# Value products by blocks of 32 queries, each with its own 128 keys, in an attention and feed-forward kernel

## The chip, the cores and the metric

The kernel runs on one core of one Trainium2 chip. The metric is the device time of one execution in microseconds (us); lower is better. The core's engines are named as the profile names them: PE (matrix products; PEld is its loading of the stationary operand), DVE and ACT (elementwise work), POOL (next to nothing here) and SP, which issues the DMA transfers here.

## The reference

Inputs and outputs are fp32. There are 8 batches of 8 heads, 512 local positions, 32 global positions, and 64 numbers per head.

```python
k_all = np.concatenate([k_g, k_l], axis=2); v_all = np.concatenate([v_g, v_l], axis=2)
out_g = np.matmul(sm(scale * np.matmul(q_g, k_all.transpose(0, 1, 3, 2))), v_all)
mask = np.abs(pos[:, None] - pos[None, :]) <= 32
s_ll = np.where(mask, scale * np.matmul(q_l, k_l.transpose(0, 1, 3, 2)), -1000000000.0)
s_lg = scale * np.matmul(q_l, k_g.transpose(0, 1, 3, 2))
a_l = sm(np.concatenate([s_lg, s_ll], axis=-1))
out_l = np.matmul(a_l, v_all)
x = np.concatenate([out_g, out_l], axis=2)        # then heads side by side: 4352 rows of 512
h = np.maximum(x @ w_in, 0.0)                     # 512 -> 2048
return h * h @ w_out                              # 2048 -> 512
```

`sm` is a softmax over the last axis. A local query sees the local keys at a distance of at most 32 and the 32 global keys. A global query sees all 544 keys.

## The kernel before, in words

**Heads and steps.** A "head" t of the kernel is one half (256 queries) of one head of one batch: 128 of them, in groups of 8 (`g = t // 8`); `hf = (t // 8) % 2` says which half of the sequence. The loop at L552 runs over steps t. Step t does the later part of head t, the scores of head t + 1 (`begin`, `rise`), and one step `m = t - 9` of the feed-forward part: `gemm1(m)` (24 passes into `h`), the square of the ReLU (`act1`, `act2`: `r`, `gh`, `gl`) and `gemm2(m - 1)` (24 passes into `o`). There are 17 blocks of 256 rows with 8 such steps each.

**Layout of one head.** The 256 queries are two sets u = 0, 1 of 128, and each set has a window of 224 key columns: 192 near keys and the 32 global ones, so that all columns of both windows are used. Before, the sets share the middle 64 near keys and the global keys: the row order of the keys is near 0 to 192, global, near 192 to 320, and set u takes columns 128u to 128u + 224. `raw` holds keys and queries (set u in partitions 64u to 64u + 64), `prob[t % 2]` the probabilities (128 queries x 2 x 224).

**Value products before.** `transposes` turns `prob` into `pt` by CHUNKS of keys: each set's own 128 keys, and the 96 shared keys (64 near, 32 global) of each set. `pt_evac` copies the 256 columns of `pt[0]` with ACT and of `pt[1]` with DVE to `pts`. `av` works on a pair of heads at each odd step: one product of the 96 shared keys with all 256 queries, and one product of 128 own keys for each set. The two heads of the pair write partitions 0 to 64 and 64 to 128 of `xa`, so they use the two halves of PE's columns. `x_evac` takes `xa` to `x_h` and `x_l`, the operands of `gemm1`.

**Global queries.** `g_scores` multiplies 32 global queries with each head's keys; `g_copy` (ACT) and `g_add` (DVE) put the scores in `sg`, two pieces per head where hf is 0 and three (128, 32 and 96 wide) where hf is 1. After a batch's half of heads come `g_soft` to `g_x`.

**Split numbers.** From head 16 on (`plain(t)` false) an fp32 operand is two operands (`hi`, `lo`; `x_h`, `x_l`; `gh`, `gl`) in a faster format, and three products replace one. The weights are loaded as pairs of 32-bit words (`wr`, 32 chunks of 512 KB), turned to fp32 (`wf`: ACT, then two DVE instructions each, in `w_bits`), and later split (`ws`). PLAN says in which of the first 24 steps these jobs are issued; `gemm1(m)` and `gemm2(m)` for m < 8 need the four `wf` chunks 4m to 4m + 3.

**Order.** PE's instructions stand in program order from the start, those of DVE and ACT from step 17 on (FREE). Before that, and for SP all along, a scheduler orders them by its own estimate of times. All loads go through one queue on SP: head t + 4's `raw` and `v` are asked for at step t (`load_head`), with 4 buffers for `raw` and 7 for `v`. A load waits on SP until the last use of the buffer it takes, and what stands behind it on SP waits too.

All calls of the engines go through `InOrder`, so the profile puts them under L53; groups are told apart by their tiles' names.

Of the kernel before, what the change touches and what calls it, by code (L numbers as in the profile page):

```python
# [7 lines left out]
F32 = mybir.dt.float32  # L8
# [6 lines left out]
B, H, SL, SG, D = 8, 8, 512, 32, 64  # L15
DM, DFF = 512, 2048
P = 128
HALF = 256
NGR = 2 * B
NT = NGR * H  # L20
WIN = 224
QK = WIN + P
VC = 192
NEG = -1.6e10
# [4 lines left out]
SCALE = 0.125  # L29
CHUNKS = ((0, 128), (320, 128), (128, 96), (224, 96))  # L30

# [28 lines left out]
def attention_moe(  # L60
# [10 lines left out]
    nc = tc.nc  # L71
    pe, ve, ac = InOrder(tc, nc.tensor), InOrder(tc, nc.vector), InOrder(tc, nc.scalar)
# [5 lines left out]
    pp = ctx.enter_context(tc.tile_pool(name="pp", bufs=3))  # L78
# [3 lines left out]
    pq = ctx.enter_context(tc.tile_pool(name="pq", bufs=4))  # L82
    pv = ctx.enter_context(tc.tile_pool(name="pv", bufs=7))

    heads = {}
# [9 lines left out]
    def load_head(t):  # L95
        raw = pq.tile([P, QK], F32, tag="raw", name=f"raw{t}")
        v = pv.tile([P, VC], F32, tag="v", name=f"v{t}")
        nc.sync.dma_start(raw, qk[t])
        nc.sync.dma_start(v, vv[t])
        heads[t] = dict(raw=raw, v=v)  # L100

# [17 lines left out]
    ident, masks = con[:, :P], con[:, P:]  # L119
# [58 lines left out]

    def g_parts(t):
        h4, grp = t % 4, (t // 4) % 2  # L180
        s = heads[t]["s"]
        if (t // 8) % 2 == 0:
            parts = ((0, 0, 0, 128), (1, 0, 128, 160))
        else:
            parts = ((0, 0, 288, 128), (1, 0, 416, 32), (1, 64, 448, 96))
        r = slice(32 * h4, 32 * h4 + 32)
        return [(sg[r, grp, d : d + n], s[u][:, WIN + o : WIN + o + n]) for u, o, d, n in parts]

    def g_copy(t):
        h4 = t % 4  # L190
        r = slice(32 * h4, 32 * h4 + 32) if plain(t) else slice(32, 64)
        for dst, src in g_parts(t):
            ac.copy(dst, src[r])

    def g_add(t):
        if plain(t):
            return
        for dst, src in g_parts(t):
            ve.tensor_add(dst, src[:32], dst)

# [50 lines left out]

    def av(t):
        pair = [heads[t], heads[t + 1]]
        for i in range(3):
            for e, hd in enumerate(pair):
                v, pts, o = hd["v"], hd["pts"], xa[half(e), :HALF]
                if i == 0:
                    pe.matmul(o, v[:96, 128:192], pts[:96, 2:4, :], start=True, stop=False, skip_group_check=True)
                else:
                    u = i - 1  # L260
                    pe.matmul(
                        o[:, P * u : P * u + P],
                        v[:, half(u)],
                        pts[:, u, :],
                        start=False,
                        stop=i == 2,
                        skip_group_check=True,
                    )

# [282 lines left out]
    for t in range(NSTEP + LAG + 1):  # L552
        m = t - LAG
        ve.on, ac.on, pe.on = [t >= x for x in FREE]
        prev, run, live, more = 1 <= t <= NT, 0 <= m < NSTEP, t < NT, t + 1 < NT
        pair = t - 3 if t % 2 and 3 <= t <= NT + 1 else None
        if t + 4 < NT:
            load_head(t + 4)
        if t % 4 == 0 and t + 4 < NT:
            g_load(t + 4)  # L560
# [37 lines left out]
        if live and t % 4 == 3 and (t // 8) % 2 == 1:  # L598
            d = t if t % 8 == 3 else t + 1
# [101 lines left out]
```

## Time and profile before

| | us |
|---|---|
| median of 3 runs (1072.8 to 1074.93) | 1072.96 |
| profiled execution | 1072.53 |
| its span, first to last instruction | 1070.7 |
| PE busy in the span | 1038.6 |
| DVE busy | 665.9 |
| ACT busy | 545.4 |

A row of the timeline has start, time covered, engine, line, operation, output and inputs, and the count of instructions; what stands in brackets is how long the engine was idle before it, and who ended that. The trace shows an fp32 product as two passes (two loads and two matmuls). Instructions on different parts of PE run side by side, so the time covered by several is less than the sum of their durations. A row of the chain has start, duration and what ran.

### The profile page before, as it was taken

The numbers are of one execution on the slowest core, as the hardware profiler recorded it, in microseconds if no ns is written. First come the engines' busy times: TensorE is split into PE (matmuls) and PEld (weight loads), VectorE is DVE, ScalarE is ACT, GpSimd is POOL, SyncE is SP. The second block draws the span as 40 slices with busy tenths as digits, with TensorE's granted clock in tenths as the row PEclk, the third lists the DMA queues.
The fourth block names the chain that finished last, engine by engine and source line by source line (L and its number), as shares of the span: only waits on it lengthen the run. The fifth ranks groups of instructions, "written<-read, shape, count | busy, mean of one in ns | idle before, by whom it ended". The sixth has DMA issues, their size and how long they took to land.

```text
span 1070.7 us, 21923 instructions
## 1 busy us (share of the span) xinstructions
PE 1038.6 (97%) x8320; PEld 868.7 (81%) x8320; DVE 665.9 (62%) x2340; ACT 545.4 (51%) x1617; POOL 0.5 (0%) x5
## 2 busy tenths in 40 slices
PE   5899889999999999999999999999999999999998
PEld 4766678888888888888888888888888888888897
DVE  5895576666666666666666666666666666653321
ACT  5886555555455445555454555554555554542222
POOL 0000000000000000000000000000000000000000
PEclk9899899999999999999999999999999999999999
DMA  8891111221221221122211221212221221101000
GB/s 266 300 331 50 51 55 42 62 61 58 66 65 36 63 83 46 58 63 62 66 58 38 69 74 46 66 44 74 66 62 39 69 73 46 39 1 45 1 21 21
DMA packets 72458, 75.88 MB, mean 71 GB/s; under 512 B 6304, under 2 KB 63776, under 8 KB 72352
## 3 DMA queue, kind: packets, MB, share of 16 engines
q1 hardware_dynamic: 72352, 74.47, 23.0%
q8 instruction: 66, 1.08, 0.4%
q14 instruction: 40, 0.33, 0.1%
HBM read 65.54 MB, written 8.91 MB: 70 GB/s over the span
## 4 chain that ended last, share of the span: by engine, by line
DVE 38%; PE 28%; ACT 24%; issue 7%; DMA 1%; SPq 0%; ACTq 0%
PE h L53 12%; PE o L53 11%; DVE prob L53 8%; ACT prob L53 7%; DVE r L53 6%; DVE gl L53 6%; ACT gh L53 5%; ACT r L53 5%; ACT sg L53 4%; DVE st L53 4%; DVE lo L53 4%; DVE pts L53 3%; PE xa L53 2%; DVE xg L53 2%; PE sb L53 2%
## 5 line engine op out<-in xcount | busy, mean ns | idle before, releaser
L53 PE MATMUL h<-x_h,ws 128*128 128x256 f32 x2048 | 401.7, 289 | 3.1 <-DVE r L53 3.1
L53 PEld LDWEIGHTS h<-x_h,ws 128*128 128x128 f32 x2048 | 327.9, 192 | 19.3 <-DVE r L53 5.6
L53 PE MATMUL o<-ws,gh 128*128 128x512 f32 x1024 | 321.3, 394 | 5.0 <-ACT ot L53 5.0
L53 PE MATMUL h<-x_l,ws 128*128 128x256 f32 x1024 | 290.7, 284 | 0.1
L53 ACT ACTIVATE prob<-prob,st 128x224 f32<-128x224 f32 x256 | 121.4, 475 | 285.9 <-DVE st L53 285.7
L53 PEld LDWEIGHTS o<-ws,gh 128*128 128x128 f32 x1024 | 184.3, 189 | 39.3 <-ACT ot L53 6.8
L53 PE MATMUL o<-ws,gl 128*128 128x512 f32 x512 | 201.8, 394 | 0.0
L53 PEld LDWEIGHTS h<-x_l,ws 128*128 128x128 f32 x1024 | 196.1, 192 | 2.1 <-DVE x_l L53 1.6
L53 DVE TENSOR_TENSOR sg<-sb,sg 32x128 f32<-32x128 f32 (+3 forms) x280 | 60.1, 257 | 143.0 <-ACT sg L53 142.8
L53 DVE TENSOR_TENSOR gl<-r,gh 128x512 fp32r<-128x512 f32 x128 | 88.6, 692 | 87.7 <-ACT gh L53 87.7
L53 DVE TENSOR_TENSOR r<-h,r 128x512 f32<-128x512 f32 x128 | 88.4, 691 | 87.8 <-ACT r L53 87.7
L53 ACT CAST gh<-r 128x512 fp32r<-128x512 f32 x128 | 79.3, 620 | 97.5 <-DVE r L53 97.5
L53 PEld LDWEIGHTS o<-ws,gl 128*128 128x128 f32 x512 | 96.4, 188 | 22.4
L53 ACT ACTIVATE r<-h 128x512 f32<-128x512 f32 x136 | 81.2, 597 | 60.3 <-PE h L53 57.5
L53 DVE CUSTOM_DVE_ANT_0 prob<-sb,con 128x224 f32<-128x224 f32 x248 | 86.1, 384 | 5.2 <-PE sb L53 5.2
L53 DVE TENSOR_SCALAR prob<-prob,st 128x224 f32<-128x224 f32 x256 | 74.5, 333 | 4.3
L53 PEld LDWEIGHTS xa<-pts,v 128*64 128x64 f32 (+1 forms) x768 | 46.7, 139 | 34.7 <-issue 23.9
L53 PEld LDWEIGHTS pt<-con,prob 64*128 64x128 f32 (+1 forms) x1024 | 41.7, 134 | 39.4 <-issue 15.7
L53 PE MATMUL xa<-pts,v 128*64 128x128 f32 (+1 forms) x768 | 72.3, 324 | 0.0
L53 PE MATMUL pt<-con,prob 64*128 64x64 f32 (+1 forms) x1024 | 60.3, 237 | 11.0 <-DVE prob L53 11.0
L53 DVE TENSOR_TENSOR lo<-raw,hi 128x352 fp32r<-128x352 f32 x112 | 58.1, 519 | 9.6 <-ACT hi L53 9.6
L53 ACT COPY sg<-sb 32x128 f32<-32x128 f32 (+3 forms) x312 | 57.8, 238 | 11.2 <-DVE st L53 8.1
(69 smaller groups left out, 1031.1 us busy)
## 6 DMA issues: line engine op xcount, KB each, us to landing
raw<-in_qk_dram SPq DMA_DIRECT2D x128, 176.0 KB, 2.3
wr<-in_w_dram SPq DMA_DIRECT2D x32, 512.0 KB, 6.0
v<-in_vv_dram SPq DMA_DIRECT2D x128, 96.0 KB, 2.0
gv<-in_vg_dram SPq DMA_DIRECT2D x32, 320.0 KB, 3.6
out_dram<-ot SPq DMA_DIRECT2D x32, 256.0 KB, 2.2
qr<-in_qg_dram SPq DMA_DIRECT2D x32, 64.0 KB, 1.8
out_dram<-ot SPq DMA_DIRECT2D x8, 64.0 KB, 1.7
con<-in_consts_dram SPq DMA_DIRECT2D x1, 288.0 KB, 3.2
```

Of the source, the lines that this page charges most:

```text
L53: r = method(*args, **kwargs)
```

## The change

Each set of 128 queries is cut into four blocks of 32. The keys of set u are laid out as near 0 to 96, global, near 96 to 192, so that block j of 32 queries finds all that it sees, 96 near keys and the 32 global ones, in the 128 columns from 32j on. A value product is then one product of 128 keys with 32 queries, with no sum over several products. `v` holds the eight blocks' values, 128 x 512 instead of 128 x 192, so near values stand in it up to four times and global ones eight times.

- `av`: 16 products of 32 columns per pair of heads in place of 2 of 256 and 4 of 128.
- `transposes`: still 8 per head, all of 128 columns (before: four of 128 and four of 96).
- `pt_evac`: 128 columns on each engine instead of 256. The two memsets of `pt` go.
- `g_scores`: 160 columns for both sets (before 128 and 160). `g_parts`: always two pieces.
- `v` is asked for at the start of step t instead of t - 4, with 4 buffers.
- Masks, keys and the values of the global part (`vg`) are laid out on the host to fit.

```diff
-VC = 192
+VC = 512
+BLK = 32
...
-    pv = ctx.enter_context(tc.tile_pool(name="pv", bufs=7))
+    pv = ctx.enter_context(tc.tile_pool(name="pv", bufs=4))
...
     def load_head(t):
         raw = pq.tile([P, QK], F32, tag="raw", name=f"raw{t}")
+        nc.sync.dma_start(raw, qk[t])
+        heads[t] = dict(raw=raw)
+
+    def load_v(t):
         v = pv.tile([P, VC], F32, tag="v", name=f"v{t}")
-        nc.sync.dma_start(raw, qk[t])
         nc.sync.dma_start(v, vv[t])
-        heads[t] = dict(raw=raw, v=v)
+        heads[t]["v"] = v
...
-    for x in pt:
-        nc.vector.memset(x[96:, 128:256], 0.0)
...
-                r, ks = half(u), slice(32, 160 + 32 * u)
-                o = hd["s"][u][:, WIN : WIN + 128 + 32 * u]
+                r, ks = half(u), slice(32, 192)
+                o = hd["s"][u][:, WIN : WIN + 160]
...
-        for i, (o, n) in enumerate(CHUNKS):
+        for i in range(2):
             for u in range(2):
-                r = half(u)
-                pe.transpose(pt[u][:n, 64 * i : 64 * i + 64], pr[r, o : o + n], ident[r, r])
+                for r in range(2):
+                    o, c = WIN * u + BLK * (2 * r + i), 2 * u + 1 - i
+                    pe.transpose(
+                        pt[r][:, 64 * c : 64 * c + 64], pr[half(r), o : o + P], ident[half(r), half(r)]
+                    )
...
-        pts = pp.tile([P, 4, P], F32, tag="pts", name=f"pts{t}")
-        ac.copy(pts[:, :, :64], pt[0][:, :256].rearrange("p (c n) -> p c n", c=4))
-        ve.tensor_copy(out=pts[:, :, 64:], in_=pt[1][:, :256].rearrange("p (c n) -> p c n", c=4))
+        pts = pp.tile([P, 2, 2, 64], F32, tag="pts", name=f"pts{t}")
+        for r, copy in enumerate((ac.copy, ve.tensor_copy)):
+            copy(pts[:, r], pt[r][:, :256].rearrange("p (u n) -> p u n", u=2)[:, :, BLK : BLK + 64])
...
-        pair = [heads[t], heads[t + 1]]
-        for i in range(3):
-            for e, hd in enumerate(pair):
...
+        for n in range(8):
+            u, j = divmod(n, 4)
+            c = BLK * (1 - j % 2)
+            for e in range(2):
+                hd = heads[t + e]
+                pe.matmul(
+                    xa[half(e), BLK * n : BLK * n + BLK],
+                    hd["v"][:, 64 * n : 64 * n + 64],
+                    hd["pts"][:, j // 2, u, c : c + BLK],
+                    start=True,
+                    stop=True,
+                    skip_group_check=True,
+                )
...
+        if live:
+            load_v(t)
         if t % 4 == 0 and t + 4 < NT:
```

The scheduler answers to this with another order in the first steps. On SP, at the program's start, the first four heads' `v` stood between the other loads and ahead of the weights `wr0`:

```order
L98 DMA raw0_85<-in_qk_dram 128x352
L99 DMA v0_86<-in_vv_dram 128x192
L108 DMA qr0_89<-in_qg_dram 128x128
L115 DMA con_91<-in_consts_dram 128x576
L98 DMA raw1_93<-in_qk_dram 128x352
L99 DMA v1_94<-in_vv_dram 128x192
L98 DMA raw2_97<-in_qk_dram 128x352
L99 DMA v2_98<-in_vv_dram 128x192
L98 DMA raw3_101<-in_qk_dram 128x352
L99 DMA v3_102<-in_vv_dram 128x192
L115 DMA con_91<-in_consts_dram 128x448
L362 DMA wr0_120<-in_w_dram 128x1024
```

The same stretch of SP's order in the changed kernel:

```order
L97 DMA raw0_85<-in_qk_dram 128x352
L111 DMA qr0_87<-in_qg_dram 128x128
L118 DMA con_89<-in_consts_dram 128x576
L97 DMA raw1_91<-in_qk_dram 128x352
L97 DMA raw2_93<-in_qk_dram 128x352
L97 DMA raw3_95<-in_qk_dram 128x352
L118 DMA con_89<-in_consts_dram 128x448
L367 DMA wr0_110<-in_w_dram 128x1024
```

Four loads fewer stand ahead of `wr0`; `v0` now follows behind `wr3` and head 4's `raw`.

On DVE, between the first part of head 5's softmax (`ISA prob1`, `st5`) and the scaling of head 4's probabilities (`prob0`) for which PE waits at 27.84 us, three instructions that turn weights (`wf`) stood before:

```order
L53 ISA prob1_111,st5_306<-s5_1_294,con_91 128x224
L53 ISA st5_306 128x1
L53 SCALAR_TENSOR_TENSOR wf2_277<-wr3_126,wf2_277 128x512
L53 TENSOR_SCALAR st4_266<-st4_266 128x2
L53 TENSOR_SCALAR st5_306<-st5_306 128x2
L53 TENSOR_SCALAR wf4_433<-wf4_433 128x512
L53 RECIPROCAL st4_266<-st4_266 128x2
L53 SCALAR_TENSOR_TENSOR wf4_433<-wr4_199,wf4_433 128x512
L53 TENSOR_SCALAR prob0_110<-prob0_110,st4_266 128x224 x2
```

The same place on DVE in the changed kernel:

```order
L53 ISA prob1_103,st5_306<-s5_1_294,con_89 128x224
L53 ISA st5_306 128x1
L53 RECIPROCAL st4_266<-st4_266 128x2
L53 TENSOR_SCALAR wf2_277<-wf2_277 128x512
L53 TENSOR_SCALAR prob0_102<-prob0_102,st4_266 128x224 x2
L53 TENSOR_SCALAR st5_306<-st5_306 128x2
L53 SCALAR_TENSOR_TENSOR wf2_277<-wr3_116,wf2_277 128x512
```

One of the three is left there; the others have moved behind the scaling. Up to head 8's copy `pts8`, which DVE does at the step of `gemm1(0)`, 10 chunks of weights have been turned before and 7 in the changed kernel.

More of the change, by code (lines that the diff above doesn't have):

```diff
@@ L29 @@
 SCALE = 0.125
-CHUNKS = ((0, 128), (320, 128), (128, 96), (224, 96))
 PLAN = [",,,b", ",,,b", ",,,b", ",,,b", ",,,b", ",,,b", ",,,b", ",,,b", "b,b,b,b", "b,bb,bbb,bb", "b,bb,bbb,bb", "b,bb,bbbs,bbs", "b,bb,bbbs,bbs", "bs,bb,bbbs,bbs", "bs,bb,bbbs,bbs", "b,bb,bbss,bs", "s,s,s,", "s,,s,s", "s,,s,s", "s,,s,", "s,,s,", "s,,s,", "s,,s,", "s,,s,"]
@@ L177, in g_scores, with g_parts @@
                     pe.matmul(o[:32], qz[r, h4, :32], hd["lo"][r, ks], start=False, stop=True, skip_group_check=True)
-    def g_parts(t):
-        h4, grp = t % 4, (t // 4) % 2
+    def g_parts(t, r):
+        h4, grp, hf = t % 4, (t // 4) % 2, (t // 8) % 2
         s = heads[t]["s"]
[L182 to L187, printed above, removed]
+        d = sg[32 * h4 : 32 * h4 + 32, grp]
+        parts = []
+        for u in range(2):
+            if u == 0 and hf == 0:
+                parts.append((d[:, :160], s[u][r, WIN : WIN + 160]))
+            else:
+                o = 256 * hf + 128 * u + 32
+                src = s[u][r, WIN : WIN + 192].rearrange("p (c n) -> p c n", c=2)[:, :, :64]
+                parts.append((d[:, o : o + 128].rearrange("p (c n) -> p c n", c=2), src))
+        return parts
     def g_copy(t):
@@ L191, in g_copy @@
         r = slice(32 * h4, 32 * h4 + 32) if plain(t) else slice(32, 64)
-        for dst, src in g_parts(t):
-            ac.copy(dst, src[r])
+        for dst, src in g_parts(t, r):
+            ac.copy(dst, src)
     def g_add(t):
@@ L197, in g_add @@
             return
-        for dst, src in g_parts(t):
-            ve.tensor_add(dst, src[:32], dst)
+        for dst, src in g_parts(t, slice(0, 32)):
+            ve.tensor_add(dst, src, dst)
     def softmax1(t):
@@ L240, in transposes @@
         pr = prob[t % 2]
-        for i, (o, n) in enumerate(CHUNKS):
+        for i in range(2):
             for u in range(2):
-                r = half(u)
-                pe.transpose(pt[u][:n, 64 * i : 64 * i + 64], pr[r, o : o + n], ident[r, r])
+                for r in range(2):
[3 more added lines that the diff above has]
+                    )
     def pt_evac(t):
-        pts = pp.tile([P, 4, P], F32, tag="pts", name=f"pts{t}")
-        ac.copy(pts[:, :, :64], pt[0][:, :256].rearrange("p (c n) -> p c n", c=4))
-        ve.tensor_copy(out=pts[:, :, 64:], in_=pt[1][:, :256].rearrange("p (c n) -> p c n", c=4))
+        pts = pp.tile([P, 2, 2, 64], F32, tag="pts", name=f"pts{t}")
+        for r, copy in enumerate((ac.copy, ve.tensor_copy)):
+            copy(pts[:, r], pt[r][:, :256].rearrange("p (u n) -> p u n", u=2)[:, :, BLK : BLK + 64])
         heads[t]["pts"] = pts
     def av(t):
-        pair = [heads[t], heads[t + 1]]
-        for i in range(3):
-            for e, hd in enumerate(pair):
[L256 to L268, printed above, removed]
+        for n in range(8):
[11 more added lines that the diff above has]
+                )
     def x_evac(t):
@@ L646 @@
     qk = np.zeros((B, 2, H, P, QK), f4)
-    vv = np.zeros((B, 2, H, P, VC), f4)
+    vv = np.zeros((B, 2, H, P, 8, D), f4)
     qt = q_l.transpose(0, 1, 3, 2)
@@ L654 @@
     for hf in range(2):
-        kw = kt[..., 256 * hf : 256 * hf + 320]
-        qw = qt[..., 256 * hf : 256 * hf + 256]
-        qk[:, hf, :, :64] = np.concatenate([kw[..., :192], kgt, qw[..., :128]], axis=-1)
-        qk[:, hf, :, 64:] = np.concatenate([kw[..., 128:192], kgt, kw[..., 192:], qw[..., 128:]], axis=-1)
-        vw = vp[:, :, 256 * hf : 256 * hf + 320]
-        vv[:, hf, :, :, :64] = vw[:, :, 0:128]
-        vv[:, hf, :, :, 64:128] = vw[:, :, 192:320]
-        vv[:, hf, :, :64, 128:] = vw[:, :, 128:192]
-        vv[:, hf, :, 64:96, 128:] = v_g
+        for u in range(2):
+            o = 256 * hf + 128 * u
+            kw, vw = kt[..., o : o + 192], vp[:, :, o : o + 192]
+            qk[:, hf, :, 64 * u : 64 * u + 64] = np.concatenate(
+                [kw[..., :96], kgt, kw[..., 96:], qt[..., o : o + 128]], axis=-1
+            )
+            seq = np.concatenate([vw[:, :, :96], v_g, vw[:, :, 96:]], axis=2)
+            for j in range(4):
+                vv[:, hf, :, :, 4 * u + j] = seq[:, :, BLK * j : BLK * j + P]
     qk, vv = qk.reshape(NT, P, QK), vv.reshape(NT, P, VC)
@@ L668 @@
     pad = np.zeros((B, H, 96, D), f4)
-    va = np.concatenate([v_l[:, :, :160], v_g, v_l[:, :, 160:], pad], axis=2)
+    va = np.concatenate([v_l[:, :, :64], v_g, v_l[:, :, 64:], pad], axis=2)
     va = va.reshape(B, 4, 2, SL + SG + 96, D)
@@ L673 @@
     qpos = np.arange(P)[:, None]
-    blocks = np.arange(-32, 288)
-    keys = np.concatenate([blocks[:192], np.full(32, 10000), blocks[192:]])
+    win = np.arange(-32, 160)
+    win = np.concatenate([win[:96], np.full(32, 10000), win[96:]])[None, :]
     masks = []
@@ L678 @@
         for u in range(2):
-            kpos = keys[128 * u : 128 * u + WIN][None, :]
-            inside = (kpos + 256 * hf >= 0) & (kpos + 256 * hf < SL)
-            ok = (kpos == 10000) | (inside & (np.abs(qpos + 128 * u - kpos) <= 32))
+            pos = win + 256 * hf + 128 * u
+            ok = (win == 10000) | ((pos >= 0) & (pos < SL) & (np.abs(qpos - win) <= 32))
             masks.append(np.where(ok, 0.0, NEG).astype(np.float32))
```

## The prediction

> **What bounds the kernel now.** I read the page's busy times first, then the chain of waits for the first 100 us, the timeline of one pair of steps, the groups by form, and the list of waits.
>
> ```profile
> PE 1038.6 (97%) x8320; PEld 868.7 (81%) x8320; DVE 665.9 (62%) x2340; ACT 545.4 (51%) x1617; POOL 0.5 (0%) x5
> 20.00:30.00 10.00, 8.10 (x73) 6.45 (x71) 8.91 (x35) 8.63 (x28) 0.00 (x0) 0.91 0.78 255
> 30.00:43.00 13.00, 11.25 (x90) 8.71 (x86) 10.97 (x45) 9.56 (x34) 0.00 (x0) 0.68 0.82 265
> 61.00:70.00 9.00, 9.00 (x44) 5.74 (x43) 8.86 (x25) 7.61 (x21) 0.00 (x0) 1.00 1.05 385
> 650.00:900.00 250.00, 248.33 (x2104) 210.32 (x2103) 162.72 (x594) 129.71 (x400) 0.00 (x0) 1.00 0.21 60
> ```
>
> The last four are windows (stretch; length; busy PE, PEld, DVE, ACT, POOL; granted clock; DMA share; GB/s). PE is the bound from about 43 us on: in the long window it lacks 1.7 of 250 us, while DVE and ACT are about two thirds and half busy. Up to 43 us it isn't: PE is 81% to 87% busy and DVE 84% to 89%.
>
> Rows of the timeline and the chain show what PE does with the work that is changed:
>
> ```profile
> 605.64 0.20 PEld L53 LDWEIGHTS xa<-pts,v 96*64 96x64 f32 x4 [0.37 <-issue]
> 605.64 1.09 PE L53 MATMUL xa<-pts,v 96*64 96x256 f32 x12
> 606.67 0.45 PE L53 MATMUL pt<-con,prob 64*128 64x64 f32 x8
> 606.92 0.35 PE L53 MATMUL sb<-hi 64*128 64x224 f32 x2
> 54.87 1.02 PE xa L53 x12
> 98.92 1.24 PE xa L53 x20
> 43.05 3.65 PE h L53 x16
> L53 PEld LDWEIGHTS xa<-pts,v 96*64 96x64 f32 x256 | 13.1, 138 | 25.0 <-issue 22.8 <-ACT r L53 2.2
> L53 PEld LDWEIGHTS pt<-con,prob 64*128 64x128 f32 x512 | 27.7, 140 | 39.4 <-issue 15.7 <-DVE prob L53 12.3 <-ACT r L53 5.2
> L53 PEld LDWEIGHTS pt<-con,prob 64*96 64x96 f32 x512 | 25.1, 128 | 0.0
> ```
>
> One pair's value products hold PE for 1.02 us, from their first load to the first transpose. The 12 passes are 6 rounds of two, since the two heads of the pair sit in different halves of PE's columns and run side by side. The row of 20 passes (the global queries' products, 10 rounds of 128 columns) takes 1.24 us. If a round costs in proportion to its columns, the 12 passes are worth 8 rounds of 128 (two of 256 count double), so two rounds are 0.22 us: 0.11 us for 128 columns, and 1.02 - 0.88 = 0.14 us are the ends (the first load, and draining before the transposes). So a round of 256 or 128 columns is set by its columns, and the next round's load lies under it.
>
> **The change, part by part.**
>
> *Value products (PE).* After, 16 rounds of 32 columns. By the columns alone a round would be 0.11 / 4 = 0.03 us, but each needs a fresh load of 64 columns of v per head. Four loads cover 0.20 us in the first row and one takes 0.138, so the second pair of loads starts some 0.06 us after the first, while it can't have waited for anything but the first pair. The transposes agree: four rounds from 606.67 to 606.92, 0.0625 us each with the first load in it. So the load sets the round. I take 0.057, just under these roundings; the bounds are 0.050 and 0.0625. The ends hold the first load, so the slot is 0.14 + 15 x 0.057 + 0.03 = 1.02 us, as before: what is saved in columns is paid in loads. With 64 pairs the bounds give -6 and +6 us; I take +0.5.
>
> Here a rule speaks against the change. The Trainium skill, "TensorE: Matmul & The Clock Gate", section "The mechanism", says that a load overlaps matmuls in flight only where their row groups differ; all of these use all rows. By it, a round would be load plus columns, 0.057 + 0.028, and the slot 0.14 + 15 x 0.085 + 0.03 = 1.45 us, +27 us in all. The trace disagrees: with loads added, the six rounds of before would take 0.14 + 0.88 + 5 x 0.057 = 1.3 us, not the 1.02 us shown.
>
> *Transposes (PE).* Two of four rounds load 128 columns, not 96: the two PEld rows differ by 12 ns, so at most 2 x 0.012 x 128 = 3 us, and nothing where the 64 moving columns already cover the load. I take +1. `g_scores`' wider set runs beside the other, which was 160 wide already: 0.
>
> *Copies and adds (DVE, ACT).*
>
> ```profile
> L53 DVE COPY pts<-pt 128x256 f32<-128x256 f32 x128 | 53.1, 415 | 8.1 <-PE pt L53 7.8
> L53 DVE COPY gp<-sb 128x64 f32<-128x64 f32 x16 | 3.4, 213 | 0.0
> L53 ACT COPY pts<-pt 128x256 f32<-128x256 f32 x128 | 47.7, 373 | 5.2 <-PE pt L53 5.0
> L53 ACT COPY gp<-sb 128x64 f32<-128x64 f32 x16 | 3.7, 230 | 0.0
> L53 ACT COPY sg<-sb 32x128 f32<-32x128 f32 x124 | 31.7, 256 | 10.7 <-DVE st L53 8.1
> L53 ACT COPY sg<-sb 32x96 f32<-32x96 f32 x64 | 14.6, 228 | 0.0
> L53 ACT COPY sg<-sb 32x32 f32<-32x32 f32 x64 | 11.0, 172 | 0.4
> PEld h L53 <- DVE r L53: 5.6, 13, 0.5
> PEld o L53 <- ACT ot L53: 6.8, 8, 2.2
> PEld sb L53 <- DVE sg L53: 5.1, 9, 3.0
> ```
>
> Between 256 and 64 columns the copies differ by 202 and 143 ns, so 128 columns cost 280 and 278 ns: 135 less on DVE and 95 less on ACT, per head. Three pieces of scores become two in 64 heads: 256 + 228 + 172 - 2 x 256 = 144 ns less on ACT, and about as much on DVE. That is 128 x 0.135 + 56 x 0.14 = 25 us of DVE and 21 us of ACT, nearly all of it beside PE's work, where it is worth nothing. It counts where PE waits for the end of a row of DVE and ACT work: the last three rows are the largest such waits once the feed-forward part runs, 17.5 us in 30 waits. A row of work that is 0.135 us shorter takes that from each wait: 30 x 0.135 = 4 us at most. Several waits share one row of work, so I take -2 (bounds -4 and 0).
>
> *The start (SP, DVE).*
>
> ```profile
> 5.92 2.08 SPq L362 DMA_DIRECT2D wr<-in_w_dram  x4
> 12.32 0.66 ACT L53 ACTIVATE wf<-wr 128x512 f32<-128x512 f32 x1 [2.62 <-DMA wr<-in_w_dram]
> 14.88 0.83 PE L53 MATMUL pt<-con,prob 64*128 64x64 f32 x8 [7.39 <-DVE prob L53]
> 27.84 0.83 PE L53 MATMUL pt<-con,prob 64*128 64x64 f32 x8 [1.88 <-DVE prob L53]
> 34.58 0.77 PE L53 MATMUL pt<-con,prob 64*128 64x64 f32 x8 [1.72 <-DVE prob L53]
> L53 DVE SCALAR_TENSOR_TENSOR wf<-wr,wf 128x512 int32<-128x512 int32 x32 | 21.9, 688 | 0.4
> L53 DVE TENSOR_SCALAR wf<-wf 128x512 int32<-128x512 int32 x32 | 13.2, 420 | 3.5 <-ACT wf L53 3.5
> 1.19 0.42 SPq L99 DMA_DIRECT2D v<-in_vv_dram  x1
> 10.00:20.00 10.00, 5.12 (x40) 4.27 (x42) 5.97 (x24) 5.44 (x17) 0.00 (x0) 1.00 0.96 352
> v<-in_vv_dram SPq DMA_DIRECT2D x128, 96.0 KB, 2.0
> raw<-in_qk_dram SPq DMA_DIRECT2D x128, 176.0 KB, 2.3
> gv<-in_vg_dram SPq DMA_DIRECT2D x32, 320.0 KB, 3.6
> ```
>
> PE's first transposes wait until 14.88 us for a row of work that begins when the first weights land at 12.3. Ahead of these, SP issues four `v` loads fewer: 4 x 0.47 us of issuing, or 384 KB, 1.1 us at the 352 GB/s of the fifth window. I take -1.4. Later PE waits 1.88 and 1.72 us for DVE. In the first of these gaps stand three instructions on weights, 0.688 + 0.420 + 0.688 = 1.8 us, and one of 0.42 after. Up to `pts8` three chunks of weights (3 x 1.11 us) and 9 x 0.135 us of copies are gone from ahead of the first `gemm1`: 4.5 us of DVE, more than the 3.6 us that PE waits. I take -2.6 of these 3.6, since DVE is not the only one late. What moves behind must be done under the feed-forward steps, where PE takes about 9.2 us a step and DVE has the slack that the window of 90 to 110 us shows:
>
> ```profile
> 90.00:110.00 20.00, 20.00 (x146) 13.61 (x144) 5.97 (x26) 8.61 (x25) 0.00 (x0) 1.00 0.19 52
> ```
>
> Against that, a `v` is 160 KB larger. Nine of 256 KB instead of thirteen of 96 KB by the first `gemm1` are 1.06 MB, 3 us of a busy DMA at 352 GB/s; the share of about 0.8 leaves room for most of it. I take +1 (bounds 0 and +4, since from 61 to 70 us the DMA is full). Together the start gives -3, bounds -6 and +3.
>
> *Loads of v later on.* From `raw`'s 2.3 us at 176 KB and `gv`'s 3.6 at 320 KB a load of 256 KB lands in about 3 us. It is asked for at step t and used at t + 2 at the earliest, two steps of some 7 us: 0. On SP it waits for the value products of heads t - 4 and the one beside it, done at step t - 1; behind it stand `raw` loads that have two steps of slack, and results.
>
> *Sum:* +0.5 + 1 - 2 - 3 = -3.5 us from 1072.53 (span 1070.7 and 1.8 around it) is 1069.0. The median of the runs is 0.4 above the profiled execution, so 1069.5.
>
> **The rivals.**
>
> 1. A round takes longer than its load. Each holds two loads and two matmuls, four instructions in 0.057 us, and 16 such rounds follow each other. For it: nothing in the trace is so dense for so long, the transposes' four rounds being the nearest. Against: these run at nearly that rate. It decides from 0.061 us on, where the slot grows by 4 us over all pairs and the gain is gone. At 0.075 the slot is 1.30 us: 64 x 0.28 = +18, less 5 and plus 1, 1087. If the two halves' loads went one after the other, 0.11 a round would give 1121; that second pair of loads after 0.06 us speaks against it. With the page's rule (not borne out above), 1096.
> 2. The start does not shorten: larger `v` loads keep the DMA full and delay weights for which DVE and ACT wait in order. For it: 0.96 and 1.05 of DMA share in two windows. Against: only one wait of ACT for weights, 2.62 us. With 0 for the start, 1072.5: no change.
> 3. Loads hide and columns set the round: 0.14 + 16 x 0.03 = 0.62 us a slot, 64 x 0.40 = -26 us, 1044. Against: the second pair of loads, which starts late.
>
> **Chances and range.** The forecast has 0.58 (own range 1064 to 1073); rival 1 0.18, of which the page's rule has 0.04; rival 2 0.20; rival 3 0.04. A measurement here can tell about 0.2%, 2.1 us. Faster takes rival 3 and all of the forecast but its upper end, 0.58; the rest of the forecast and most of rival 2 are the same, 0.22; rival 1 and what is left of rival 2 are slower, 0.20. The range of 1062 to 1080 takes in the forecast with a start of -6 and waits of -4, rival 2, and the mild part of rival 1.
>
> **What would show it.** The slot of `xa` in the timeline: 1.02 us says that the load sets the round, 0.6 rival 3, 1.3 or more rival 1. The first `gemm1` at about 40 us instead of 43.05, and the gaps ahead of the transposes at 28 and 35 us gone, show the start. The three waits for `r`, `ot` and `sg` should be 2 us less in sum. Waits for DMA on PE, DVE or ACT before 100 us would show rival 2. The forecast is wrong if a round is over 0.061 us, or if work on weights moved behind the first `gemm1` makes PE wait there.

## The result, and the profile after

| | before | changed |
|---|---|---|
| median, us (range of 4 runs each) | 1073.9 (1072.8 to 1074.93) | 1062.53 (1060.88 to 1064.94) |
| ratio of the times, 95% interval | | 0.9896 (0.9873 to 0.9919) |
| profiled execution, us | 1072.53 | 1062.88 |
| its span, us | 1070.7 | 1061.1 |
| granted clock over the span | 0.990 | 0.987 |

The change makes the kernel 11.4 us faster in the medians and 9.65 us in the profiled executions; the forecast was 3.5 faster, with a range down to 1062. What follows goes by the profiled executions.

The changed kernel's page, first row, and its windows over the stretches that were shown of before:

```profile
PE 1033.5 (97%) x9600; PEld 885.9 (83%) x9600; DVE 647.1 (61%) x2282; ACT 531.0 (50%) x1553; POOL 0.5 (0%) x5
```

```profile
20.00:30.00 10.00, 6.35 (x118) 5.35 (x118) 8.62 (x43) 7.88 (x28) 0.00 (x0) 1.00 0.95 313
30.00:43.00 13.00, 12.54 (x94) 10.47 (x94) 11.25 (x45) 9.29 (x31) 0.00 (x0) 0.61 0.94 330
61.00:70.00 9.00, 9.00 (x72) 6.18 (x68) 8.44 (x24) 7.01 (x18) 0.00 (x0) 1.00 0.98 335
650.00:900.00 250.00, 249.32 (x2428) 216.49 (x2426) 158.29 (x578) 127.34 (x390) 0.00 (x0) 1.00 0.26 80
```

PE is still the bound, and in the long window it now lacks 0.7 of 250 us where it lacked 1.7. That is a hint only: matmuls overlap in the records, so that a wait of 0.3 us need not leave a hole in PE's busy time. A better measure is when PE starts a given step. Rows of the timeline of before, and then of the changed kernel: the first pass of `gemm1(17)` and of `gemm1(121)`.

```profile
189.82 0.39 PE L53 MATMUL h<-x_h,ws 128*128 128x256 f32 x1
975.52 0.28 PE L53 MATMUL h<-x_h,ws 128*128 128x256 f32 x1
```

```profile
186.90 0.39 PE L53 MATMUL h<-x_h,ws 128*128 128x256 f32 x1
965.54 0.28 PE L53 MATMUL h<-x_h,ws 128*128 128x256 f32 x1
```

At step 17 the changed kernel is 2.9 us ahead and at step 121 it is 10.0 ahead; to the end little more happens (the spans differ by 9.6). So 7 of the 10 us come from the 104 steps between, at a granted clock of 1.00: 1.84 us in the first 16 steps and then, evenly, 1.1 in each 16 up to step 113. From step 49 to step 113 a period of 16 steps (one batch) takes 121.39 us before and 120.30 after. The forecast looked for most of its gain in the start.

In the pair's rows of the changed kernel's timeline, the value products' slot runs from their first load to the first transpose:

```profile
598.91 1.01 PEld L53 LDWEIGHTS xa<-pts,v 128*64 128x64 f32 x32 [0.37 <-ACT gh L53]
598.91 1.13 PE L53 MATMUL xa<-pts,v 128*64 128x32 f32 x32
599.97 0.46 PE L53 MATMUL pt<-con,prob 64*128 64x64 f32 x8
600.24 0.35 PE L53 MATMUL sb<-hi 64*128 64x224 f32 x2
```

It is 1.06 us here and 1.056 in the median of 56 pairs, against 1.023 before: 0.033 us more. The 32 loads are 16 rounds of two, and their 1.01 us, less one load of 0.14, gives 0.058 us a round. The transposes take 0.271 us instead of 0.258 in the median.

The groups by form, and from the page the loads of `v`:

```profile
L53 DVE COPY pts<-pt 128x128 f32<-128x128 f32 x128 | 36.2, 283 | 6.7 <-PE pt L53 6.7
L53 ACT COPY pts<-pt 128x128 f32<-128x128 f32 x128 | 34.1, 266 | 12.1 <-PE pt L53 11.8
```

```profile
v<-in_vv_dram SPq DMA_DIRECT2D x128, 256.0 KB, 2.9
```

A copy costs 283 and 266 ns instead of 415 and 373: 132 and 107 less. A load of `v` lands in 2.9 us.

Which of PE's waits changed is read from the list of waits of PE's loads between step 17 and step 121. Four rows of before (waits in all, times, longest):

```profile
PEld h L53 <- DVE r L53: 5.5, 12, 0.5
PEld o L53 <- ACT ot L53: 2.5, 6, 0.4
PEld sb L53 <- DVE sg L53: 1.8, 7, 0.3
PEld h L53 <- DVE x_l L53: 1.1, 6, 0.2
```

And in the changed kernel the one row that is left of them:

```profile
PEld h L53 <- DVE r L53: 4.4, 12, 0.4
```

The other three, 5.4 us in 19 waits of 0.28 us on average, are gone altogether. Most of them come six times, about once in a period of 16 steps. (Waits of 0.37 us ahead of `xa` and of 0.17 or 0.37 ahead of `pt` are in the list too; gaps of the same length stand before these loads where no engine is named, so they tell nothing of lost time.)

### The profile page after: what moved, and what is told of

The parts are those of the page before. It is cut to its first block, busy times and chain, and to the rows that moved or that the text cites. A ratio compares the mean times of both kernels' runs of the same rounds, so it can differ in the third digit from the quotient of the medians.

```text
span 1061.1 us, 24289 instructions
## 1 busy us (share of the span) xinstructions
PE 1033.5 (97%) x9600; PEld 885.9 (83%) x9600; DVE 647.1 (61%) x2282; ACT 531.0 (50%) x1553; POOL 0.5 (0%) x5
## 4 chain that ended last, share of the span: by engine, by line
PE 69%; DVE 16%; ACT 10%; issue 3%; DMA 1%; SPq 0%; ACTq 0%
PE h L53 30%; PE o L53 26%; PE xa L53 6%; PE sb L53 4%; DVE prob L53 3%; PE pt L53 3%; ACT prob L53 3%; DVE r L53 3%; DVE gl L53 2%; ACT r L53 2%; ACT gh L53 2%; DVE xg L53 2%; ACT sg L53 2%; DVE st L53 2%; DVE lo L53 1%
## 5 line engine op out<-in xcount | busy, mean ns | idle before, releaser
L53 DVE TENSOR_TENSOR sg<-sb,sg 32x160 f32<-32x160 f32 (+1 forms) x224 | 55.6, 284 | 144.5 <-ACT sg L53 144.3
L53 PEld LDWEIGHTS xa<-pts,v 128*64 128x64 f32 x2048 | 66.3, 140 | 25.0 <-issue 19.5
L53 PE MATMUL xa<-pts,v 128*64 128x32 f32 x2048 | 73.4, 226 | 0.0
L53 PE MATMUL pt<-con,prob 64*128 64x64 f32 x1024 | 60.1, 237 | 9.8 <-DVE prob L53 9.8
L53 PEld LDWEIGHTS pt<-con,prob 64*128 64x128 f32 x1024 | 43.1, 140 | 30.8 <-issue 14.0
L53 DVE TENSOR_TENSOR lo<-raw,hi 128x352 fp32r<-128x352 f32 x112 | 58.1, 519 | 9.8 <-ACT hi L53 9.8
L53 ACT COPY sg<-sb 32x128 f32<-32x128 f32 (+1 forms) x248 | 54.5, 261 | 16.4 <-DVE st L53 13.3
```

The costliest lines, as they stand in the source:

```text
L53: r = method(*args, **kwargs)
```

## The experiments

A start of "step 17" below is the first pass of `gemm1(17)`. "Period" is the mean of four periods of 16 steps, from `gemm1(49)` to `gemm1(113)`. The first two experiments are single profiled runs. The others have intervals against runs of the kernel before on the same chip, whose medians were 1072.6 to 1074.5 us. The times of steps are those of the one profiled execution of each kernel. The period repeats to 0.1 us between kernels that differ in other things (120.29 to 120.30, 121.33 to 121.44), while what is gained up to step 17 holds to 1 or 2 us only, for a reason that comes at the end. Of the kernels made for the experiments, all but three (changed with the third piece, before with late `v`, changed with `lo` on POOL) leave part of the result out or take wrong columns for it; they serve for times alone.

| kernel | median us | ratio to before (95%) | first `gemm1` | step 17 | period | step 121 |
|---|---|---|---|---|---|---|
| before | 1073.9 | | 42.98 | 189.82 | 121.39 | 975.52 |
| changed | 1062.53 | 0.9896 (0.9873 to 0.9919) | 38.17 | 186.90 | 120.30 | 965.54 |
| changed, 64 columns a product | 1063.18 | | 39.73 | 186.25 | 120.44 | 965.83 |
| changed, loads of 32 columns | 1048.85 | | 36.96 | 182.03 | 118.89 | 951.45 |
| changed, small `v` | 1063.91 | 0.9901 (0.9887 to 0.9916) | 39.35 | 187.62 | 120.29 | 966.19 |
| small `v`, long copies | 1073.39 | 1.0001 (0.9990 to 1.0013) | 41.39 | 190.72 | 121.38 | 975.88 |
| small `v`, long copies, third piece | 1077.4 | 1.0035 (1.0019 to 1.0050) | 42.02 | 193.05 | 121.59 | 980.18 |
| changed, third piece | 1063.97 | 0.9916 (0.9893 to 0.9940) | 38.34 | 187.33 | 120.29 | 966.10 |
| before, late `v` | 1072.16 | 0.9996 (0.9984 to 1.0007) | 41.68 | 189.29 | 121.44 | 975.32 |
| before, short copies | 1063.46 | 0.9908 (0.9888 to 0.9928) | 43.48 | 189.35 | 120.01 | 966.49 |
| before, DVE's copy short | 1065.55 | 0.9926 (0.9898 to 0.9954) | 44.68 | 190.72 | 120.12 | 968.50 |
| before, ACT's copy short | 1071.52 | 0.9989 (0.9974 to 1.0004) | 42.21 | 188.96 | 121.33 | 974.39 |
| before, short copies, late `v` | 1064.18 | 0.9919 (0.9895 to 0.9943) | 43.94 | 189.81 | 120.01 | 966.94 |
| changed, `lo` on POOL | 1055.72 | 0.9846 (0.9820 to 0.9872) | 37.93 | 183.00 | 119.71 | 958.08 |

### What sets a round of value products: 64 columns a product, and loads of 32 columns

The first takes twice the columns through each load, the second loads half as many columns of `v`.

```diff
-                    xa[half(e), BLK * n : BLK * n + BLK],
+                    xa[half(e), BLK * min(n, 6) : BLK * min(n, 6) + 64],
                     hd["v"][:, 64 * n : 64 * n + 64],
-                    hd["pts"][:, j // 2, u, c : c + BLK],
+                    hd["pts"][:, j // 2, u, :],
```

> The changed kernel with value products of 64 columns instead of 32, so with the same 32 loads of 64 columns per pair of heads and twice the moving columns (the values in xa are then not the reference's). The changed kernel's slot of xa is 1.056 us, 0.0585 us a round. Theory 1, the load sets the round and the columns lie under it: still 0.058 a round, slot 1.06 to 1.09, time as the changed kernel's 1062.5. Theory 2, a round is load plus columns one after the other (0.03 + 0.03): 0.085 a round, slot 1.47, 64 x 0.41 = 26 us more, 1089. Theory 3, four instructions a round limit it: as theory 1.

```diff
+    nc.vector.memset(xa, 0.0)
...
-                    xa[half(e), BLK * n : BLK * n + BLK],
-                    hd["v"][:, 64 * n : 64 * n + 64],
+                    xa[64 * e : 64 * e + 32, BLK * n : BLK * n + BLK],
+                    hd["v"][:, 64 * n : 64 * n + 32],
```

> The changed kernel with loads of 32 columns of v instead of 64 (only the first 32 of each head's 64 numbers are computed), same count of instructions and same 32 moving columns. Theory 1, the load sets the round: about 0.03 us a round, slot 0.14 + 15 x 0.03 + 0.03 = 0.62 us, 64 x 0.43 = 28 us less, 1035. Theory 2, load plus columns: 0.015 + 0.03, slot 0.85, 13 us less, 1049. Theory 3, four instructions a round are the limit: slot stays 1.06, 1062.5.

A pair in the timeline of the kernel with 64 columns a product:

```profile
598.75 1.15 PE L53 MATMUL xa<-pts,v 128*64 128x64 f32 x32
599.83 0.46 PE L53 MATMUL pt<-con,prob 64*128 64x64 f32 x8
```

And of the kernel with loads of 32 columns:

```profile
604.22 0.59 PEld L53 LDWEIGHTS xa<-pts,v 128*32 128x32 f32 x32 [0.36 <-issue]
604.86 0.46 PE L53 MATMUL pt<-con,sg 64*128 64x64 f32 x8
```

Twice the columns lengthen the slot from 1.056 to 1.083 us in the median, 0.027 once a pair: what is added is the tail of the last round, and in 15 rounds the 64 columns lie wholly under the next load. Half the load, with the columns and the count of instructions as they were, shortens the slot to 0.629 (0.64 in the rows): 0.59 us less a load of 0.11 over 15 intervals is 0.032 us a round. So the load sets the round, and neither the columns nor the rate at which four instructions can be issued does. The rule of the Trainium skill, "TensorE: Matmul & The Clock Gate", "The mechanism", that a load overlaps matmuls in flight only where their row groups differ, is not what this kernel does: all these products use all rows, and the loads lie over the columns all the same, since 32 columns more in every round add 0.027 us to the slot and not 15 times that.

The second kernel also missed what its slots promised. 64 slots are 0.427 us shorter, 27 us, but the time is 14 us below the changed kernel's and the period only 1.41 us below, where eight slots freed 3.4. Its 1048.85 us is what the second theory gave, but with a slot of 0.85 us; the slot of 0.629 rules that theory out, and the time met it by chance. From step 17 to step 121 the slots free 22.2 us and 9.2 arrive. In its list of waits over these steps, the three that the changed kernel had lost are back, and the one for `r`, 4.4 us there, has grown:

```profile
PEld h L53 <- DVE r L53: 6.8, 18, 0.4
PEld sb L53 <- DVE sg L53: 3.2, 13, 0.3
PEld h L53 <- DVE x_l L53: 2.8, 7, 0.4
PEld o L53 <- ACT ot L53: 1.7, 6, 0.3
```

These are 10.1 us more than in the changed kernel, of the 13 that are missing. PE got faster and met the rows of DVE and ACT. So these rows, with DVE 61% busy in the changed kernel, bind nearly as tightly as PE.

### The size of the loads: small `v`

```diff
-        v = pv.tile([P, VC], F32, tag="v", name=f"v{t}")
-        nc.sync.dma_start(v, vv[t])
+        v = pv.tile([P, 192], F32, tag="v", name=f"v{t}")
+        nc.sync.dma_start(v, vv[t][:, :192])
...
-                    hd["v"][:, 64 * n : 64 * n + 64],
+                    hd["v"][:, 64 * (n % 3) : 64 * (n % 3) + 64],
```

> The changed kernel with v loaded as 192 columns (96 KB, as before the change) and the products taken from these 192, so that only the size of the loads and of the v tiles differ (the values are not the reference's). Theory start-DMA, larger v loads hold back the first 43 us: the first gemm1 comes 1 to 3 us earlier than the changed kernel's 38.2 us, time 1060 to 1061.5. Rival, the larger loads are hidden: 1062.5 within 0.5, the 16 steps of a batch stay 120.3 us.

96 KB a head instead of 256 change nothing that can be told: 0.9901 against 0.9896, a period of 120.29 against 120.30, and a first `gemm1` no earlier (39.35 against 38.17). The 20 MB more of DMA are free. This kernel also leaves room in SBUF for longer copies, which the changed kernel doesn't, so it is the base of the next two.

### The copies put back: long copies, and a third piece

Both engines copy all 256 columns of `pt` again; then `g_parts` gives three pieces for half of the heads, as before (128, 64 and 64 columns here, 128, 32 and 96 before). `av` reads the same columns from the longer tile.

```diff
-        pts = pp.tile([P, 2, 2, 64], F32, tag="pts", name=f"pts{t}")
+        pts = pp.tile([P, 2, 256], F32, tag="pts", name=f"pts{t}")
...
-            copy(pts[:, r], pt[r][:, :256].rearrange("p (u n) -> p u n", u=2)[:, :, BLK : BLK + 64])
+            copy(pts[:, r], pt[r][:, :256])
```

```diff
+                if u == 1 and hf == 1:
+                    parts.append((d[:, o : o + 64], s[u][r, WIN : WIN + 64]))
+                    parts.append((d[:, o + 64 : o + 128], s[u][r, WIN + 96 : WIN + 160]))
+                    continue
```

Long copies alone:

> As the run with small v loads, but pt_evac copies all 256 columns on each engine; the global scores stay in two pieces. If theory A holds, the copies (135 ns of DVE and 95 of ACT in every head) count for about two thirds and the pieces (137 and 144 ns in every second group of 8 heads) for a third: 16 steps of a batch about 121.0 us, time 5 to 7 us above the run with small v. Rival: the pieces alone matter, since they stand where the waits are; then 120.3 us and no difference.

Long copies and the third piece:

> As the run with small v loads, but with DVE and ACT given back the work that the change took: pt_evac copies all 256 columns on each engine, and the global scores of heads with hf = 1 go in three pieces. Products, transposes and loads are as in the run with small v. Theory A, PE's waits at the end of rows of DVE and ACT work carry from step to step, and the shorter copies took them away: 16 steps of a batch go from 120.3 back to 121.5 or more (before: 121.39), and the whole time is 8 to 11 us above the run with small v. Rival B, the waits went for another reason (the order of the transposes, the products of 32): 120.3 us, time within 2 us of the run with small v.

The third piece alone, on the changed kernel:

> The changed kernel with the global scores of heads with hf = 1 in three pieces again (128, 64 and 64 columns on ACT and DVE), results unchanged. Theory A: about a third of the 10 us of waits come back, 16 steps of a batch about 120.7, time 1065 to 1066. Rival, the copies of pt alone matter: 120.3, 1062.5.

The long copies give back everything, 9.5 us against the kernel with small `v`, where 5 to 7 were expected: the time is that of before (1.0001), and so is the period, 121.38. By the steps, 6.6 us of this come from step 17 to step 121 and 3.1 up to step 17. The third piece is worth nothing by itself (1063.97, period 120.29) and about 4 us on top of the long copies (1077.4, period 121.59); of these, 2.0 us come from step 17 to step 121, where it costs 0.1 by itself, and the rest before. So a stretch of work of the same length costs next to nothing where the rows have slack and costs time where they are already late. The two cuts are not two terms that can be added.

### The copies alone, in the kernel before

The kernel before, with its value products, its transposes, its pieces and its early `v`. Each engine copies 128 columns instead of 256, and the product of the shared keys reads the columns that were copied.

```diff
-        pts = pp.tile([P, 4, P], F32, tag="pts", name=f"pts{t}")
-        ac.copy(pts[:, :, :64], pt[0][:, :256].rearrange("p (c n) -> p c n", c=4))
-        ve.tensor_copy(out=pts[:, :, 64:], in_=pt[1][:, :256].rearrange("p (c n) -> p c n", c=4))
+        pts = pp.tile([P, 2, P], F32, tag="pts", name=f"pts{t}")
+        ac.copy(pts[:, :, :64], pt[0][:, :128].rearrange("p (c n) -> p c n", c=2))
+        ve.tensor_copy(out=pts[:, :, 64:], in_=pt[1][:, :128].rearrange("p (c n) -> p c n", c=2))
...
-                    pe.matmul(o, v[:96, 128:192], pts[:96, 2:4, :], start=True, stop=False, skip_group_check=True)
+                    pe.matmul(o, v[:96, 128:192], pts[:96, 0:2, :], start=True, stop=False, skip_group_check=True)
```

> The kernel before with pt_evac copying 128 of 256 columns on each engine (the shared keys' product reads the own keys' part instead, so the values are not the reference's); products, transposes, pieces and loads as before. Theory A: the waits of PE shrink without any other part of the change: 16 steps of a batch 120.5 to 120.9 instead of 121.39, and the start some 1 us shorter: 1073.9 less 4 to 7 us, 1067 to 1070. Rival B: 121.4 us and 1073.

This has the whole gain: 1063.46, ratio 0.9908, with a first `gemm1` no earlier than before (43.48). Rows of its list of waits from step 17 to step 121:

```profile
PEld h L53 <- DVE r L53: 5.1, 12, 0.5
PEld o L53 <- ACT ot L53: 0.2, 1, 0.2
```

Of the three rows that the changed kernel lost, one wait is left here. And its steps 17 and 121 in the timeline:

```profile
189.35 0.39 PE L53 MATMUL h<-x_h,ws 128*128 128x256 f32 x1
966.49 0.29 PE L53 MATMUL h<-x_h,ws 128*128 128x256 f32 x1
```

Then one engine's copy at a time, with the other left as it was (the product of the shared keys again reads the columns that were copied):

```diff
-        ve.tensor_copy(out=pts[:, :, 64:], in_=pt[1][:, :256].rearrange("p (c n) -> p c n", c=4))
+        ve.tensor_copy(out=pts[:, :2, 64:], in_=pt[1][:, :128].rearrange("p (c n) -> p c n", c=2))
```

> The kernel before with the DVE half of pt_evac alone copying 128 instead of 256 columns (135 ns less per head; values not the reference's). The copies on both engines gave 120.01 us for 16 steps against 121.39. If the rows of work run through DVE's copy (DVE is the busier engine, and its copy stands between x_l and the softmax), 120.1 us and 1064 to 1066. If ACT's copy counts as much, about 120.7 and 1068.

```diff
-        ac.copy(pts[:, :, :64], pt[0][:, :256].rearrange("p (c n) -> p c n", c=4))
+        ac.copy(pts[:, :2, :64], pt[0][:, :128].rearrange("p (c n) -> p c n", c=2))
```

> The kernel before with the ACT half of pt_evac alone copying 128 instead of 256 columns (95 ns less per head; values not the reference's). If the rows of work run through DVE's copy, 121.3 us for 16 steps and 1071 to 1073. If ACT's copy counts as much, about 120.7 and 1068.

DVE's copy alone shortens the period by 1.27 us (120.12) and ACT's by 0.06 (121.33). So it is DVE's row that PE waited for. With DVE's copy alone short, the list of waits from step 17 to step 121 also loses those that end on ACT's `ot` (its copy of `o`, on the way out), all but one, though ACT's copy is as long as before; `sg` and `x_l` are gone and `r` is as it was:

```profile
PEld h L53 <- DVE r L53: 5.5, 12, 0.5
PEld o L53 <- ACT ot L53: 0.2, 1, 0.2
```

Sixteen copies that are 0.132 us shorter take 2.1 us of DVE out of a period, and 1.27 of them arrive at PE.

### When `v` is asked for

```diff
-    pv = ctx.enter_context(tc.tile_pool(name="pv", bufs=7))
+    pv = ctx.enter_context(tc.tile_pool(name="pv", bufs=4))
...
+        if live:
+            load_v(t)
```

> The kernel before with its v loads (still 96 KB) asked for at step t with 4 buffers, as in the change, and nothing else changed. Theory, the start gained from the v loads leaving the way of the first weights: the first weights land 1 to 2 us earlier than 12.3 us, the first gemm1 starts 1 to 3 us earlier than 43.05, time 1071 to 1073 against 1073.9. Rival, the start gained only from the shorter DVE work and another order of it: first gemm1 at 43, time 1073.9.

> The kernel before with the late v loads (96 KB, 4 buffers) and copies of 128 columns on both engines (values not the reference's); products, transposes and pieces as before. The scheduler puts 10 chunks of weights ahead of head 8's copy, as before, not the changed kernel's 7. Theory, the first gemm1 comes as early as DVE has few chunks ahead of it: 41 to 42 us, not 38; 16 steps 120.0; time 1061.5 to 1063. Rival, late v and short copies themselves make the start short: 38 to 39 us, time 1059 to 1060.

In the kernel before, asking for `v` four steps later is worth nothing that can be told (0.9996), though the first weights come at 10.86 us instead of 12.32 and the first `gemm1` at 41.68 instead of 42.98; by step 17 0.5 us of that is left. With the short copies as well (1064.18) it is no better than the short copies alone, and the first `gemm1` is at 43.94, later than either expectation had it. In all these kernels the first `gemm1` goes with how many chunks of weights DVE turns ahead of head 8's copy: 7 in the changed kernel, the one with a third piece, the one with loads of 32 columns and the one with `lo` on POOL (36.96 to 38.34 us), 8 with small `v` and with 64 columns (39.35, 39.73), 10 in before, with long copies, and in all other kernels made from before (41.39 to 44.68). That the number of chunks sets it was not tested by itself. Which part of the change makes the scheduler hold three chunks back was not isolated either: late `v` and short copies don't do it by themselves, but the long copies put back in the kernel with small `v` take it from 8 chunks to 10, so the short copies seem to be needed for it along with something else.

### A version that is faster: `lo` on POOL

If DVE's row is what PE waits for, other work taken off it should help the changed kernel too. `lo`, the difference of an operand and its `hi`, is 0.519 us in each of 112 heads; POOL does nothing here.

```diff
-        ve.tensor_sub(lo, hd["raw"], f(hi))
+        nc.gpsimd.tensor_sub(lo, hd["raw"], f(hi))
```

> The changed kernel with the low part of keys and queries (lo = raw - hi, 519 ns of DVE per head from head 16 on) computed by POOL, which is idle; results unchanged. If PE's remaining waits (0.58 us per 16 steps, and some 12 us between 110 and 160 us) still end on rows of DVE work, 16 steps go to 119.8 or less and the time to 1055 to 1059. Rival: POOL takes far longer, or holds DVE up where both work in SBUF, and PE waits for lo at the next scores: 1063 or more.

1055.72 us, 0.9846 of before: 6.8 us below the changed kernel, with nothing left out. The long window of this kernel, and then its whole list of waits of PE's loads from step 17 to step 121 for a named engine:

```profile
650.00:900.00 250.00, 250.00 (x2462) 217.69 (x2460) 156.21 (x546) 128.96 (x391) 31.89 (x33) 1.00 0.27 82
```

```profile
PEld pt L53 <- ACT r L53: 2.2, 6, 0.4
PEld xa L53 <- ACT r L53: 0.4, 1, 0.4
PEld pt L53 <- ACT gh L53: 0.2, 1, 0.2
```

PE is busy for the whole of the window and none of the waits for DVE is left. The period falls by 0.59 us, to 119.71: that is 3.6 us from step 17 to step 121. Another 3.0 us come between steps 9 and 17. Windows of the changed kernel and of this one over these eight steps:

```profile
114.35:186.90 72.55, 66.51 (x593) 56.85 (x591) 49.13 (x164) 39.05 (x110) 0.00 (x0) 0.91 0.22 69
113.45:183.00 69.55, 64.14 (x593) 55.03 (x591) 47.68 (x154) 37.43 (x108) 7.64 (x8) 0.95 0.24 72
```

PE's longest wait for `sg` falls from 2.89 to 1.98 us there, but only 0.6 of the 3.0 us is less idle time. The other 2.4 are the same 593 matmuls done in less busy time, at a granted clock of 0.95 instead of 0.91. Whether the clock was higher because PE waited less is not shown.

This kernel also gives an estimate of what PE loses in a period elsewhere, since it loses next to nothing: 120.30 - 119.71 = 0.59 us in the changed kernel. In the kernel before, slots and transposes take 8 x 0.033 + 16 x 0.013 = 0.47 us less, so that it would need 119.24 and loses 2.15; with short copies it loses 0.77. Over the 6.5 periods from step 17 to step 121 these are 3.8, 14.0 and 5.0 us.

## Why the prediction was right in direction and too small

The 1062.53 us lie just inside the range that reached to 1062, and below the forecast's own range of 1064 to 1073. That the range held is luck: its lower end was there for -6 in the start and -4 in the waits, and the runs gave -2.5 and -9. By its own steps, with steps 17 and 121 as marks, the 9.98 us at step 121 split in three. From before to before with short copies is the copies' part: 975.52 - 966.49 = 9.03. From there to the changed kernel is the rest: by step 17 it is 189.35 - 186.90 = 2.45 ahead, and over steps 17 to 121 it takes 778.64 us instead of 777.14, 1.50 longer.

| step | forecast | measured |
|---|---|---|
| value products and transposes | +1.5 | +1.5 from step 17 to step 121, where their slots add 3.1 |
| PE's waits at the end of DVE's and ACT's rows | -2 (bounds -4 and 0) | -9.0 |
| the start | -3 (bounds -6 and +3) | -2.5 (to 1 or 2 us) |
| `v` larger and later | 0 (and +1 in the start) | 0 |

**Value products: right in what sets the round, too small in size.** The load sets the round, at 0.058 us for a forecast of 0.057. The slot came out 0.033 us above before instead of equal, 2.1 us over 64 pairs; the transposes' 0.013 us over 128 heads are 1.7, inside the bound of 3. Together they are 3.8 us on PE where 1.5 was forecast. From step 113 to step 121 this cost stands by itself: these eight steps take 56.63 us with the old products and 56.84 with the new ones, with long copies as with short ones, and four slots and eight transposes would give 0.24. Over steps 17 to 121 it would be 3.1 us, of which 1.5 show in PE's steps: the changed kernel waits for `r` 0.7 us less than before with short copies does, and the third piece is gone too, so part of it seems to have been taken from time in which PE would have waited. Rival 1 decided from 0.061 us a round and did not come true. Rival 3, columns setting the round, is out by both runs on the round. (Two of the rivals' sums are a microsecond off, 1121 for 1120 and 1044 for 1043; nothing rests on that.)

**The waits: the step that failed.** The mechanism was right, that a shorter row ends PE's waits for it, but the price was more than four times too small, and its bound was no bound. "30 x 0.135 = 4 us at most" did two things wrong. It took the list as all that PE loses: between steps 17 and 121 its three rows (`r`, `ot`, `sg`) hold 9.8 us, where PE loses 14.0 by the estimate above. And it let each wait shrink once, by one copy. The 19 waits that vanished were 0.28 us each, twice what one copy gives. The likely reason is that DVE works its row in order, and what it is late by at one step it is still late by at the next until there is slack, so that the 0.132 us of several heads are taken from one wait. A better bound was at hand: 16 x 0.135 = 2.2 us of DVE in a period, 14 us over the 104 steps, up to what PE loses there. The text gave the 25 us of DVE as "nearly all of it beside PE's work, where it is worth nothing"; about a third of them counted. Of the 9.0 us, 8.6 come from step 17 to step 121; in the changed kernel with small `v` the same copies are worth 6.6 over these steps, so the size depends on what else is in the row. That the copies are the cause is shown, by putting them back (1.0001), and that it is mostly DVE's, by cutting it alone (0.9926). That lateness is carried from step to step is inferred, from these sizes and from the third piece, which costs 0.1 us on short copies and 2.0 on long ones over these steps.

**The start: right in size by luck, with other terms.** Rows of the chain of the changed kernel (start, duration, what ran):

```profile
12.33 0.83 PE pt L53 x5
38.24 5.13 PE h L53 x16
```

And one of its timeline, the largest gap of PE's loads between 13 and 38 us:

```profile
29.64 0.51 PEld L53 LDWEIGHTS pt<-con,prob 64*128 64x128 f32 x8 [1.47 <-DVE prob L53]
```

The first transposes come 2.55 us earlier for a forecast of 1.4, and the first `gemm1` at 38.2 for a forecast of 40. Of the two gaps that were to go, the one at 35 us is gone and the one at 28 us is a little shorter, and PE waits some 1.2 us at 20, 24 and 26 us instead. But the first `gemm1` now takes 5.13 us, not 3.65. Windows of the changed kernel show why, and the third is of before:

```profile
34.00:38.00 4.00, 4.00 (x50) 3.40 (x48) 3.39 (x15) 2.91 (x10) 0.00 (x0) 0.50 0.88 284
38.00:43.40 5.40, 5.40 (x20) 4.14 (x20) 4.57 (x17) 2.79 (x8) 0.00 (x0) 0.70 1.02 402
43.05:46.70 3.65, 3.65 (x19) 2.96 (x20) 3.45 (x14) 3.50 (x13) 0.00 (x0) 1.00 0.75 245
```

The granted clock is half just before it and 0.70 during it; before, `gemm1(0)` ran at 1.00. In all fourteen kernels the time of the first `gemm1` (3.72 to 6.14 us from its first matmul to the end of its last) times the granted clock over it is 3.67 to 3.72, so the clock accounts for nearly all of the difference. Of 4.8 us 3.3 are left at step 1 and 2.9 at step 17. So the start gave 3 us for 3, by +1.5 that the forecast had not seen and about -1.5 that it had not seen either.

The clock also limits what can be said of the start's parts. From 20 to 45 us it was 0.80 in the kernel with small `v` and 0.52 in the one with long copies; over steps 9 to 17 it was 0.91 in the changed kernel and 0.95 in before with short copies, which is 1.1 us faster there. So part of each difference up to step 17 is clock, and why it fell in one kernel and not in another was not tested.

**Rival 2: no.** The DMA did get fuller, 0.95 and 0.94 from 20 to 43 us against 0.78 and 0.82, but ACT's 2.62 us for the first weights are gone, and DVE's first masks were applied at 5.33 us against 5.45 before. The waits of PE's loads that end on a DMA rise from 4.8 to 5.9 us before 100 us; with small `v` they are 4.7, and the first `gemm1` is no earlier for it. So the +1 for a busier DMA is there in the waits and doesn't show in the time.

**No wait behind the first `gemm1`.** The weights that moved behind it did not hold PE up: the 3.3 us at step 1 are still 3.1 at step 9 (117.43 to 114.35), and the 0.24 between is what the value products and transposes of eight steps cost more.

## What to carry to other kernels

A PE that is 97% busy can still be paced by an in-order engine at 62%: look for many small waits that recur once a period, and compare the start times of the same step in two runs instead of busy shares. Price a cut in such a row by the work that it takes out of a whole period, with what the bound engine loses in that period as its ceiling, and not by one instruction a wait. Then test the parts alone: here the product that gave the change its name cost time, and the copy that it made shorter was the whole steady gain. And compare stretches in which the granted clock is the same.

## What the runs showed of the hardware

Two engines that do unrelated work can hold each other up. With `lo` on POOL, the groups by form show POOL's instruction at 0.975 us, where DVE took 0.519, and DVE's scaling of the probabilities longer than in the changed kernel:

```profile
L145 POOL TENSOR_TENSOR lo<-raw,hi 128x352 fp32r<-128x352 f32 x112 | 109.2, 975 | 815.8 <-ACT hi L53 815.8
L53 DVE TENSOR_SCALAR prob<-prob,st 128x224 f32<-128x224 f32 x256 | 102.0, 439 | 4.3
```

In the changed kernel that scaling takes 334 ns. Rows of the timeline of the kernel with `lo` on POOL show how it comes about, here with an instruction of two columns that mostly takes 0.17 us:

```profile
626.20 0.95 POOL L145 TENSOR_TENSOR lo<-raw,hi 128x352 fp32r<-128x352 f32 x1 [6.52 <-ACT hi L53]
626.22 0.96 DVE L53 TENSOR_SCALAR st<-st 128x2 f32<-128x2 f32 x1
```

It starts 0.02 us after POOL's and ends with it. The Trainium skill, "SBUF — State Buffer", "Who interferes with whom", says that DVE and POOL share a pair of ports as an exclusive lock, so that, where an instruction of DVE uses the pair, the later of the two is blocked for the whole instruction; these rows agree. Not every instruction of DVE is held up: the reciprocals of two columns of `st`, many of which run beside POOL too, take 0.166 us as in the changed kernel. Of the 58.1 us of `lo` that DVE no longer does, 27 and 13 come back as longer scalings (of `prob` and of `st`), and DVE's busy time falls by 6.5 us only, from 647.1 to 640.6. The waits for DVE's rows are gone all the same; where in the row the 0.519 us stood seems to count more than how much work is left, which was not tested by itself.
